# Attention by landmarks and expert layer on one core: q, k and C turned in 32x32 blocks by VectorE instead of by TensorE, scores and v product in 32x32 tiles, the pseudo-inverse carried as I-X, and a new plan of the order

## The chip, the core and the metric

The kernel runs on one core of one Trainium2 chip. The core has five engines that each work through their own queue in order: TensorE (PE in the profile, with its weight loads shown as PEld), VectorE (DVE), ScalarE (ACT), GpSimd (POOL) and SyncE (SP, which here only issues DMAs). TensorE writes its results into PSUM; VectorE and ScalarE read them there. The metric is the device time of one execution in microseconds. The kernel before takes 335.03 us, the median of three runs (333.28, 335.03 and 337.61).

## The reference

There are two parts. The first is an attention in Nyström form over 8 batches, 8 heads, 576 rows and a head size of 64, with m = 32 landmarks; a landmark is the mean of 18 successive rows.

```
q_lm = q.reshape(B, H, m, S // m, D).mean(axis=3)
k_lm = k.reshape(B, H, m, S // m, D).mean(axis=3)
A = sm(q, k_lm); Bm = sm(q_lm, k_lm); C = sm(q_lm, k)     # sm: softmax of the scaled scores
Z = Bm.T / (norm1(Bm) * norminf(Bm) + 1e-06)
for _ in range(6):
    Z = 2 * Z - Z @ Bm @ Z
attn = A @ Z @ C @ v
```

The second is an expert layer over the 4608 rows of 512 values (heads side by side). Each row goes to the one of 8 experts with the highest logit, through `relu(x @ w1[e]) @ w2[e]` (512 to 1024 to 512), and is scaled by its gate probability and by a sigmoid gate. The output is 4608 x 512 in float32.

## The kernel before

**Layout and work per half.** A batch is worked in two halves of four heads (`hf`, 16 halves in all). q, k and v of a half are loaded by one DMA each on SP (L378) into 96 partitions: partition p holds six successive rows of each of the four heads, in four pieces of 1,536 bytes. TensorE turns q and k with an identity matrix (L390: six columns of blocks, 24 transposes of 96x128 a half), and the results are copied out of PSUM by ScalarE or VectorE (`copy_to`, L345 and L351) into `Tk` and `Tq`: on partitions are then 2 rows x 64 of the head size. The sums over the 18 rows of a landmark are taken from `T` (L412 to L424: VectorE in one reduction, L414 and L417, or GpSimd in four additions, L420 to L424), the two partition halves are swapped and added (L347, L351 and L435). That gives `lm`.

The scores of C (L446) and of A (L491) are matmuls on 64x32 tiles of the array: eight calls of 288 columns, each on its own tile. For C: maximum (L452, VectorE), exponential (L455, ScalarE), six transposes of 128 columns on TensorE (L463), a copy out (ECT), and the product with v on 128x32 tiles (L475, 24 calls of 64 columns), scaled into `XW` (L481). For A: a 32x32 block transpose from PSUM by VectorE (L495), maximum (L498), subtraction on GpSimd (L503), exponential (L505), sums and reciprocal (L509, L510), product on GpSimd (L512), and the transpose back into `AT` (L516).

**Work per batch.** B's scores and softmax (L527 to L545), its column sums (L554 to L560), then the pseudo-inverse. It does not form Z; it carries `[X | Y]` per head, 32 + 64 columns, with X in the place of Z·B and Y of Z·C·v: a matmul gives `X·[X | Y]` (L573, eight calls of 96 columns on 32x32 tiles), and VectorE forms `2[X | Y] - X·[X | Y]` (L580 to L585), seven times. Then the logits (L593 to L621), the routing on VectorE (`route1` to `route4`, L637 to L686) with a count over all partitions on TensorE (`count`, L655), and x in bf16, transposed (`xT_all`, L699). The expert that most rows of the batch chose gets its weights by DMAs on GpSimd's queue (L312, L315 and L720, with a cast from float32 to bf16). Then 64 matmul calls `up` a batch (L734, 288 columns, bf16), relu by ScalarE (L343), 40 calls `down` a batch (L749, 512 columns), a scaled copy (L756 or L758) and the store on SP (L761). Rows of other experts are handled afterwards under a condition.

**What sets the order.** Nothing in this part is ordered by hand on the engines. The class `Plan` takes each piece of work as an operation (`P.op`) with the engines that may do it and a cost in nanoseconds for each, what it reads and writes, a tile form for TensorE (`mode`; a change costs `SWITCH` = 95) and a priority, and simulates a schedule once when the program is built. The operations are emitted in the order of their planned start; every engine then runs its own queue in that fixed order and waits wherever an operand is late. Priorities are about the batch number `b` plus a small step; the expert matmuls of batch `b` have `fr = b + 3.5`, so they stand behind the attention of the next three batches where both are ready. Tiles come from small pools (`tag`): three buffers each for q, k and v, two for `T`, two PSUM pairs `S`, two banks `M`, two banks `F` for the expert matmuls, one w1 and one w2 for even and one for odd batches.

Of the kernel before, what the change touches and what calls it, by code (L numbers as in the profile page):

```python
# [22 lines left out]
F32 = mybir.dt.float32  # L23
# [5 lines left out]
ADD = mybir.AluOpType.add  # L29
# [193 lines left out]
def kernel(  # L223
# [23 lines left out]
    PT = 96  # L247
# [5 lines left out]
    SHYF = 300.0  # L253
# [13 lines left out]
    ones = pool.tile([128, 128], F32, name="ones")  # L267
    e8 = pool.tile([128, E], F32, name="e8")
# [15 lines left out]
    t_s3 = tag("s3", 1, [128, HH * PT])  # L284
    t_s9 = tag("s9", 2, [128, 2, 128])
    t_lm = tag("lm", 3, [128, 2, 128])
    t_sw = tag("sw", 1, [128, 2, 128])
    t_EC = tag("EC", 1, [128, 2, U2])
    t_ECT = tag("ECT", 1, [PT, 6, 128])
# [27 lines left out]
    with tc.manual_schedule():  # L317
        nc.vector.memset(ones, 1.0)
# [9 lines left out]
        for hf in range(2):  # L328
            nc.sync.dma_start(out=wgs[hf * D:(hf + 1) * D, :, :E],
                              in_=moe_w_gate[hf * HH * D:(hf + 1) * HH * D].rearrange("(h d) e -> d h e", d=D))  # L330
            nc.sync.dma_start(out=wgs[hf * D:(hf + 1) * D, :, E:],
                              in_=moe_w_output_gate[hf * HH * D:(hf + 1) * HH * D].rearrange("(h d) e -> d h e", d=D))
        nc.vector.tensor_scalar(out=wgs[:, :, E:], in0=wgs[:, :, E:], scalar1=-1.0, scalar2=None, op0=MUL)
# [19 lines left out]

        def turned(T, x):
            if x == "k":
                return T.t.rearrange("p (j n) -> p j n", j=3)
            return T.t.rearrange("p (n j) -> p j n", j=3)

# [6 lines left out]
        xTs, coms = {}, {}  # L365

        def batch(b):
# [4 lines left out]
            vns = []  # L372
            for hf in range(2):
                pr = b + 0.1 * hf
                ns = {}
                for x, src in (("k", k), ("q", q), ("v", v)):
                    n = ns[x] = Val(t_n[x])
                    P.op({"SP": 60}, lambda e, n=n, src=src, hf=hf: nc.sync.dma_start(  # L378
                        out=n.t, in_=src[b, hf * HH:(hf + 1) * HH].rearrange("h (p t) d -> p h (t d)", t=6)),
                        w=[n[0]], prio=pr, lag=2000, load=2300)  # L380
                vns.append(ns["v"])
                Ts = {"q": Val(t_T["q"]), "k": Val(t_T["k"])}
                order = [("k", 0), ("k", 1), ("k", 2), ("q", 0), ("q", 1), ("q", 2)]
                for a in range(3):
                    tp = Val(p_S)
                    two = order[2 * a:2 * a + 2]
                    for i, (x, j) in enumerate(two):
                        def turn(e, x=x, j=j, i=i, tp=tp, n=ns[x]):
                            for h in range(HH):
                                nc.tensor.transpose(tp.t[:, i, h * PT:(h + 1) * PT],  # L390
                                                    in_=n.t[:, h, j * 128:(j + 1) * 128], identity=I128[:PT, :PT])
                        P.op({"PE": 332}, turn, r=[ns[x][0]], w=[tp[i]], hold=[Ts[y] for y, _ in two], mode=(128, 128), prio=pr + .01)
                    if two[0][0] == two[1][0]:
                        x, j = two[0]
                        T = Ts[x]
                        P.op(evac(768), copy_to(lambda T=T, j=j, x=x: turned(T, x)[:, j:j + 2],
                                                lambda tp=tp: tp.t[:, :, :HH * PT]),
                             r=[tp[0], tp[1]], w=[T[j], T[j + 1]], prio=pr + .01)
                    else:
                        for i, (x, j) in enumerate(two):  # L400
                            T = Ts[x]
                            P.op(evac(384), copy_to(lambda T=T, j=j, x=x: turned(T, x)[:, j],
                                                    lambda tp=tp, i=i: tp.t[:, i, :HH * PT]),
                                 r=[tp[i]], w=[T[j]], prio=pr + .01)
                s9 = Val(t_s9)
                for i, x in enumerate("qk"):
                    T = Ts[x]
                    s3 = Val(t_s3)

                    def sums(e, T=T, s9=s9, s3=s3, i=i, x=x):  # L410
                        f = turned(T, x)
                        if e == "DVE":  # L412
                            if x == "k":
                                nc.vector.tensor_reduce(  # L414
                                    s9.t[:, i], f.rearrange("p j (r w) -> p r j w", w=3), axis=XY, op=ADD)
                            else:
                                nc.vector.tensor_reduce(  # L417
                                    s9.t[:, i], T.t.rearrange("p (r w) -> p r w", w=9), axis=X, op=ADD)
                            return
# [14 lines left out]
                def folded(e, lm=lm, s9=s9, sw=sw):  # L434
                    (nc.gpsimd if e == "POOL" else nc.vector).tensor_tensor(lm.t, s9.t, sw.t, op=ADD)  # L435
# [409 lines left out]
```

## Time and profile before

| what | value |
|---|---|
| median of three runs | 335.03 us |
| the profiled execution | 333.46 us, of which span 331.8 us |
| PE busy | 287.8 us (87%) |
| DVE busy | 192.0 us (58%) |
| ACT busy | 174.7 us (53%) |
| POOL busy | 85.2 us (26%) |
| mean granted PE clock | 0.973 |
| read from HBM | 61.90 MB, written 9.44 MB |

"Busy" of an engine is the time in which at least one of its instructions runs; matmuls are pipelined, so a busy PE may still be waiting in part. A group line of the profile gives line, engine, operation, output<-input, shapes, count, then busy time and the mean nanoseconds of one, then the idle time of the engine just before such instructions and what ended it. In the listing by slices the span is cut in 40 equal parts (8.3 us each) and each digit is a busy share in tenths. A line of the timeline gives start and length in us, engine, line and operation, and how many instructions are merged in it. A row of the view by stretches gives the stretch, its length, and the busy time of PE, PEld, DVE, ACT and POOL in it (with instruction counts), then the granted clock, the DMA share and GB/s.

### The profile page before, as it was taken

Reading aid. Unit: us, or ns where it says so; the run is one execution under the profiler, and the core shown is the slowest. Engines: PE = TensorE matmul, PEld = TensorE weight load, DVE = VectorE, ACT = ScalarE, POOL = GpSimd, SP = SyncE. Lnnn points to the kernel's source line nnn. Section 1 sums busy time; section 2 is a strip of 40 time slices with the busy share of each in tenths; the row PEclk is TensorE's granted clock in tenths of the full one; section 3 lists DMA queues with packets and bytes.
Section 4 is the critical chain, followed back from the end, with each engine's and each line's share of the span. In section 5 each row is a group of like instructions: output and inputs, shape, how many; then the busy total and the mean of one; then the engine's idle time right before and its main releaser. Section 6 shows DMA issues by size and latency. Waiting matters only on the chain. (4 is left out here: it accounts for less than half of the span.)

```text
span 331.8 us, 10174 instructions
## 1 busy us (share of the span) xinstructions
PE 287.8 (87%) x4270; PEld 182.8 (55%) x4281; DVE 192.0 (58%) x526; ACT 174.7 (53%) x370; POOL 85.2 (26%) x126
## 2 busy tenths in 40 slices
PE   0576868799979989899978998999999998999994
PEld 0545655566656665657644575666565555454551
DVE  1258928977987388729866669784968626000000
ACT  1344526537845457537654566465764345454542
POOL 1034642237153024214331402330221311010000
PEclk9999779769999999999999999999999999999999
DMA  4999999289999978076730455665000946949103
GB/s 96 247 247 245 250 213 233 49 187 227 229 182 232 261 225 193 9 212 178 167 85 2 134 154 123 139 104 167 2 18 2 219 84 99 177 113 200 51 33 112
DMA packets 33584, 48.95 MB, mean 147 GB/s; under 512 B 2816, under 2 KB 26368, under 8 KB 33536
## 3 DMA queue, kind: packets, MB, share of 16 engines
q1 hardware_dynamic: 25536, 37.79, 44.4%
q0 software_dynamic: 8000, 10.49, 19.7%
q8 instruction: 34, 0.56, 0.7%
q14 instruction: 14, 0.11, 0.1%
HBM read 61.90 MB, written 9.44 MB: 215 GB/s over the span
## 5 line engine op out<-in xcount | busy, mean ns | idle before, releaser
L734 PE MATMUL F<-xT_all,w 128*128 128x288 bf16 x512 | 76.1, 286 | 2.1 <-ACT y L756 1.1
L749 PE MATMUL F<-w,hT 128*128 128x512 bf16 (+1 forms) x310 | 73.2, 380 | 1.0 <-ACT y L756 0.3
L734 PEld LDWEIGHTS <-w 128*128 128x128 bf16 x512 | 47.4, 98 | 24.1 <-issue 11.7
L343 ACT ACTIVATE hT<-F 128x288 bf16<-128x288 f32 x128 | 50.0, 411 | 16.8 <-PE F L734 14.9
L749 PEld LDWEIGHTS <-hT 128*128 128x128 bf16 (+1 forms) x320 | 30.7, 100 | 35.0 <-issue 2.8
L756 ACT ACTIVATE y<-F,co 128x512 f32<-128x512 f32 (+1 forms) x38 | 26.1, 686 | 42.4 <-PE F L749 36.6
L390 PE MATMUL S<-I,nk 96*128 96x96 f32 x192 | 25.2, 275 | 14.2 <-DMA nk<-in_k_dram 11.2
L573 PE MATMUL M<-X 32*32 32x96 f32 x768 | 26.5, 251 | 5.3 <-issue 3.2
L503 POOL TENSOR_TENSOR At<-At,sm 128x576 f32<-128x576 f32 x16 | 18.5, 1156 | 49.1 <-DVE sm L498 27.5
L390 PEld LDWEIGHTS S<-I,nk 96*128 96x128 f32 x192 | 21.1, 160 | 17.1 <-issue 9.0
L345 ACT COPY Tq<-S 128x768 f32<-128x768 f32 (+1 forms) x23 | 22.9, 1004 | 11.1 <-PE S L390 11.1
L390 PE MATMUL S<-I,nq 96*128 96x96 f32 x192 | 24.6, 270 | 2.1 <-DVE Tk L351 1.8
L345 ACT COPY Tk<-S 128x384 f32<-128x384 f32 (+1 forms) x25 | 15.6, 633 | 20.0 <-PE S L390 19.5
L512 POOL TENSOR_TENSOR At<-At,sm 128x576 f32<-128x576 f32 x16 | 18.5, 1159 | 28.2 <-DVE sm L510 10.3
L583 DVE SCALAR_TENSOR_TENSOR X<-X,M 128x192 f32<-128x192 f32 x40 | 13.7, 344 | 19.6 <-PE M L573 19.4
L573 PEld LDWEIGHTS M<-X 32*32 32x32 f32 x768 | 15.7, 105 | 16.7 <-issue 7.8
L417 DVE TENSOR_REDUCE s<-Tq 128x128 f32<-128x1152 f32 x14 | 18.9, 1350 | 8.8 <-ACT Tq L345 8.7
L390 PEld LDWEIGHTS S<-I,nq 96*128 96x128 f32 x192 | 20.4, 156 | 5.7 <-DVE Tk L351 2.4
L345 ACT CAST xT_all<-S 128x576 bf16<-128x576 f32 x28 | 16.7, 641 | 11.3 <-PE S L699 11.2
L455 ACT ACTIVATE EC<-S,sm 128x576 f32<-128x576 f32 x16 | 11.8, 740 | 18.3 <-DVE sm L453 16.7
L435 POOL TENSOR_TENSOR lm<-s,sw 128x256 f32<-128x256 f32 x12 | 8.7, 725 | 41.1 <-ACT sw L345 34.4
L345 ACT COPY ECT<-S 96x768 f32<-96x768 f32 x14 | 11.1, 796 | 14.9 <-PE S L463 14.8
(118 smaller groups left out, 395.0 us busy)
## 6 DMA issues: line engine op xcount, KB each, us to landing
nk<-in_k_dram SPq DMA_DIRECT2D x16, 576.0 KB, 8.8
nq<-in_q_dram SPq DMA_DIRECT2D x16, 576.0 KB, 8.4
nv<-in_v_dram SPq DMA_DIRECT2D x16, 576.0 KB, 8.0
w<-in_moe_w_dram POOLq DMA_DIRECT2D x8, 1024.0 KB
out_dram<-y SPq DMA_DIRECT2D x32, 256.0 KB, 2.7
w<-in_moe_w_dram POOLq DMA_DIRECT2D x8, 512.0 KB
w<-in_moe_w_dram POOLq DMA_DIRECT2D x16, 256.0 KB
out_dram<-y SPq DMA_DIRECT2D x8, 128.0 KB, 2.4
```

The lines of the kernel that those rows point to most:

```text
L343: nc.scalar.activation(out=dst(), in_=src(), func=RELU)
L345: nc.scalar.copy(dst(), src())
L390: nc.tensor.transpose(tp.t[:, i, h * PT:(h + 1) * PT], in_=n.t[:, h, j * 128:(j + 1) * 128], identity=I128[:PT, :PT])
L417: nc.vector.tensor_reduce(s9.t[:, i], T.t.rearrange("p (r w) -> p r w", w=9), axis=X, op=ADD)
L455: P.op({"ACT": 900}, lambda e, pC=pC, EC=EC, st=st: nc.scalar.activation(out=EC.t, in_=pC.t[:, :, :U2], func=EXP, scale=s_a, bias=st.t[:, ...
L503: P.op({"POOL": 1160}, lambda e, At=At, st=st: nc.gpsimd.tensor_tensor(At.t, At.t, b_l(st.t[:, 8:8 + g]), op=SUB), r=[st["ax"]], w=[At[0]] ...
L512: P.op({"POOL": 1160}, lambda e, At=At, st=st: nc.gpsimd.tensor_tensor(At.t, At.t, b_l(st.t[:, 32:32 + g]), op=MUL), r=[st["as"]], w=[At[0 ...
L573: nc.tensor.matmul(pN.t[r_, hf * W:(hf + 1) * W], lhsT=cur.t[r_, hf, :m], rhs=cur.t[r_, hf, :])
L583: nc.vector.scalar_tensor_tensor(out=nxt.t, in0=cur.t, scalar=2.0, in1=p3, op0=MUL, op1=SUB)
L734: nc.tensor.matmul(ph.t[:, :NH], lhsT=w1.t[:, dc, fc * 128:(fc + 1) * 128], rhs=xT.t[:, dc, n * NH:(n + 1) * NH], start=(dc == 0), stop=(d ...
L749: nc.tensor.matmul(py.t[:tk, :], lhsT=hTs[fc].t[:, i * 128:i * 128 + tk], rhs=w2.t[:, fc, :], start=(fc == 0), stop=(fc == FCH - 1))
L756: nc.scalar.activation(out=y.t[:tk], in_=py.t[:tk, :], func=COPY, scale=com.t[:tk, i:i + 1])
```

## The change

- q and k are loaded as 128 partitions (head, landmark) with 18 rows x 64 values each, 4,608 bytes in one piece. VectorE turns them in 32x32 blocks in one instruction each (L391); the head size then lies in two blocks `j` of 32. v is loaded the same way with its two partition halves exchanged, by two DMAs.
- Landmark sums are taken from the loaded rows: batch 0 on TensorE with a stack of 32x32 identities `I32s` (L404, 144 calls a half), later batches on GpSimd in five additions (L414 to L418) or VectorE in one reduction (L412). A 32x32 block transpose gives `lm` (L423 or L427). The swap and the fold go away.
- The scores of C and A become one operation of 32 calls on 32x32 tiles (L443 and L445), accumulated over `j`. C's rows are written two heads further (`o`), so both use different tiles. C's maximum stays on VectorE (L450), its scaling moves to ScalarE (L454).
- C is turned in 32x32 blocks by VectorE (L459) and the v product runs on 32x32 tiles: 72 calls of 64 columns (L468). Its scale is done by ScalarE or VectorE (L479, L481).
- The pseudo-inverse carries `[R | Y]` with R = I - X. The matmul gives `R·[R | Y]` (L565, eight calls) and a second one adds Y through the identity (L568, eight calls of 64 columns); the step is then a plain copy by ScalarE or VectorE (L582, L584). The last step does the Y columns alone.
- AT is written at steps of 18 elements (L506). The gate weights are loaded in an operation of their own, and negated on GpSimd (L386).
- The plan: `fr = b + 1.5`, new costs for loads (2050 for 2300, weights 5000 for 8100) and for the new operations.

In the built order TensorE gets, for 384 transposes of q and k and 96 of C that go away, 288 calls for sums, 1152 instead of 384 for the v product, 512 instead of 256 for the scores and 384 more in the pseudo-inverse. It changes its tile form 136 times instead of 200. The first expert matmul of batch 0 stands a few operations behind the count of batch 0, ahead of the v products of batch 2.

```diff
-    t_n = {x: tag(f"n{x}", 3, [PT, HH, 6 * D]) for x in "qkv"}
-    t_T = {x: tag(f"T{x}", 2, [128, 3 * HH * PT]) for x in "qk"}
+    t_n = {x: tag(f"n{x}", 3, [128, g, D]) for x in "qkv"}
+    t_T = {x: tag(f"T{x}", 2, [128, 2, S]) for x in "qk"}
...
+        nc.vector.tensor_reduce(I32s, I128.rearrange("p (a c) -> p c a", c=m), axis=X, op=ADD)
...
+                    def bring(e, n=n, x=x, src=src, hf=hf):
+                        rows_ = src[b, hf * HH:(hf + 1) * HH].rearrange("h (r t) d -> (h r) t d", t=g)
+                        if x != "v":
+                            nc.sync.dma_start(out=n.t, in_=rows_)
+                            return
+                        for a in range(2):
+                            nc.sync.dma_start(out=n.t[a * D:(a + 1) * D], in_=rows_[(1 - a) * D:(2 - a) * D])
...
-                        def turn(e, x=x, j=j, i=i, tp=tp, n=ns[x]):
-                            for h in range(HH):
-                                nc.tensor.transpose(tp.t[:, i, h * PT:(h + 1) * PT],
-                                                    in_=n.t[:, h, j * 128:(j + 1) * 128], identity=I128[:PT, :PT])
-                        P.op({"PE": 332}, turn, r=[ns[x][0]], w=[tp[i]], hold=[Ts[y] for y, _ in two], mode=(128, 128), prio=pr + .01)
...
+                for x in "kq":
+                    P.op({"DVE": 1370}, lambda e, T=Ts[x], n=ns[x]: nc.vector.transpose(
+                        out=T.t.rearrange("p j (t r) -> p t j r", r=m), in_=n.t.rearrange("p t (j c) -> p t j c", j=2)),
+                        r=[ns[x][0]], w=[Ts[x][0]], prio=pr + .01)
...
+                        def sums_pe(e, n=ns[x], pM=pM, i=i):
+                            for t in range(g):
+                                for h in range(HH):
+                                    r_ = slice(h * m, (h + 1) * m)
+                                    nc.tensor.matmul(pM.t[r_, i * D:(i + 1) * D], lhsT=I32s[r_, :], rhs=n.t[r_, t, :],
+                                                     start=(t == 0), stop=(t == g - 1))
+                        P.op({"PE": 1020}, sums_pe, r=[ns[x][0]], w=[pM[i], s9[i]], mode=(32, 32), prio=pr + .005)
...
+                        nc.gpsimd.tensor_tensor(s3.t, n.t[:, :9], n.t[:, 9:], op=ADD)
+                        nc.gpsimd.tensor_tensor(s3.t[:, :4], s3.t[:, :4], s3.t[:, 4:8], op=ADD)
+                        nc.gpsimd.tensor_tensor(s3.t[:, :2], s3.t[:, :2], s3.t[:, 2:4], op=ADD)
+                        nc.gpsimd.tensor_tensor(s3.t[:, 0], s3.t[:, 0], s3.t[:, 1], op=ADD)
+                        nc.gpsimd.tensor_tensor(s9.t[:, i], s3.t[:, 0], s3.t[:, 8], op=ADD)
+                    P.op({"POOL": 2850, "DVE": 1350}, sums, r=[ns[x][0]], w=[s9[i], s3[0]], prio=pr + .005, shy={"DVE": SHY})
...
+                def scores(e, pC=pC, pA=pA, lm=lm, Ts=Ts):
+                    for n in range(2):
+                        for j in range(2):
+                            for h in range(HH):
+                                r_ = slice(h * m, (h + 1) * m)
+                                o = (h + 2) % HH
+                                nc.tensor.matmul(pC.t[o * m:(o + 1) * m, n, :U2], lhsT=lm.t[r_, 0, j, :],
+                                                 rhs=Ts["k"].t[r_, j, n * U2:(n + 1) * U2], start=(j == 0), stop=(j == 1))
+                                nc.tensor.matmul(pA.t[r_, n, :U2], lhsT=lm.t[r_, 1, j, :],
+                                                 rhs=Ts["q"].t[r_, j, n * U2:(n + 1) * U2], start=(j == 0), stop=(j == 1))
+                P.op({"PE": 1050}, scores, r=[lm[0], Ts["k"][0], Ts["q"][0]], w=[pC[0], pA[0]], hold=[EC, At, st],
+                     mode=(32, 32), prio=pr + .03)
...
+                P.op({"DVE": 780}, lambda e, EC=EC, ECT=ECT: nc.vector.transpose(
+                    out=ECT.t.rearrange("p t r -> p (t r)"), in_=EC.t.rearrange("p a c -> p (a c)")),
+                    r=[EC[0]], w=[ECT[0]], prio=pr + .03)
...
-                    for c in range(6):
-                        t = 2 * (c % 3) + c // 3
+                    for t in range(g):
                         for h in range(HH):
-                            nc.tensor.matmul(pV.t[h * m:(h + 1) * m, :D], lhsT=ECT.t[:, c, h * m:(h + 1) * m],
-                                             rhs=n.t[:, h, t * D:(t + 1) * D], start=(c == 0), stop=(c == 5))
-                P.op({"PE": 850}, pv, r=[ECT[0], ns["v"][0]], w=[pV[0]], hold=[XW], mode=(128, 32), prio=pr + .04)
+                            o = (h + 2) % HH
+                            nc.tensor.matmul(pV.t[h * m:(h + 1) * m, :D], lhsT=ECT.t[o * m:(o + 1) * m, t, :],
+                                             rhs=n.t[o * m:(o + 1) * m, t, :], start=(t == 0), stop=(t == g - 1))
+                P.op({"PE": 1020}, pv, r=[ECT[0], ns["v"][0]], w=[pV[0]], hold=[XW], mode=(32, 32), prio=pr + .04)
...
-                    out=AT.t[:, :S].rearrange("p (u n) -> p n u", n=2), in_=At.t.rearrange("p (n k) r -> p n (k r)", n=2)),
+                    out=AT.t[:, :S].rearrange("p (r t) -> p t r", t=g), in_=At.t),
...
+                            nc.tensor.matmul(pN.t[r_, hf * W + lo:(hf + 1) * W], lhsT=cur.t[r_, hf, :m],
+                                             rhs=cur.t[r_, hf, lo:], start=True, stop=(it == 0))
+                            if it:
+                                nc.tensor.matmul(pN.t[r_, hf * W + m:(hf + 1) * W], lhsT=I32s[r_, :],
+                                                 rhs=cur.t[r_, hf, m:], start=False, stop=True)
...
+                P.op({"ACT": 320, "DVE": 340} if it else {"DVE": 600}, step, r=[pN[0], sb[3]] if it == 0 else [pN[0]],
+                     w=[nxt["x"], nxt["y0"], nxt["y1"]], prio=pr + .05)
...
-            fr = b + 3.5
+            fr = b + 1.5
```

More of the change, by code (lines that the diff above doesn't have):

```diff
@@ L267 @@
     ones = pool.tile([128, 128], F32, name="ones")
+    I32s = pool.tile([128, m], F32, name="I32s")
     e8 = pool.tile([128, E], F32, name="e8")
@@ new lines, in c_rec @@
+                def c_rec(e, st=st):
+                    for a in range(2):
+                        nc.vector.reciprocal(st.t[a * D:(a + 1) * D, 3:4], st.t[(1 - a) * D:(2 - a) * D, 2:3])
+                P.op({"DVE": 280}, c_rec, r=[st[1]], w=[st[2]], prio=pr + .035)
+                def pv_out(e, pV=pV, st=st, hf=hf):
+                    if e == "ACT":
+                        nc.scalar.activation(out=XW.t[:, hf, m:], in_=pV.t[:, :D], func=COPY, scale=st.t[:, 3:4])
+                    else:
+                        nc.vector.tensor_scalar(out=XW.t[:, hf, m:], in0=pV.t[:, :D], scalar1=st.t[:, 3:4],
+                                                scalar2=None, op0=MUL)
@@ L495, in batch @@
+                P.op({"ACT": 260, "DVE": 285}, pv_out, r=[pV[0], st[2]], w=[XW[f"y{hf}"]], prio=pr + .04)
                 P.op({"DVE": 800}, lambda e, pA=pA, At=At: nc.vector.transpose(
```

184 lines of the change are left out of this document (65 added, 119 removed).

## The prediction

> **What bounds the kernel now.** I read the stretches first, cut at the routing of the first and of the last batch (the count matmul L655 starts at 63.6 and 277.7 us), then the slices, the matmul rows of the timeline, and the waits.
>
> ```profile
> 0.00:63.60 63.60, 39.64 (x642) 28.12 (x643) 36.73 (x81) 27.92 (x52) 22.09 (x40) 0.93 0.91 206
> 63.60:277.70 214.10, 200.41 (x3363) 128.58 (x3370) 152.17 (x429) 121.74 (x267) 60.26 (x82) 0.98 0.62 140
> 277.70:331.80 54.10, 47.76 (x267) 26.12 (x270) 3.10 (x18) 25.02 (x53) 2.80 (x4) 0.99 0.46 107
> ```
> Columns: stretch, length, then PE, weight loads, DVE, ACT and POOL busy, clock, DMA share, GB/s. In the middle stretch PE is busy 200 of 214 us, DVE 152, ACT 122: PE sets the pace. The start is set by loads and chains; the end is expert work alone.
>
> ```profile
> PE   0576868799979989899978998999999998999994
> DVE  1258928977987388729866669784968626000000
> PEclk9999779769999999999999999999999999999999
> ```
> PE fills up only after slice 9 (first expert matmul at 79.5 us); its clock dips in slices 4 to 8.
>
> ```profile
> 75.07 0.53 PE L573 MATMUL M<-X 32*32 32x96 f32 x16
> 75.53 0.88 PE L475 MATMUL M<-nv,ECT 96*32 96x64 f32 x48
> 76.34 0.88 PE L390 MATMUL S<-I,nk 96*128 96x96 f32 x8
> 82.96 0.74 PE L699 MATMUL S<-AT,X 32*64 32x288 f32 x16
> 85.03 0.72 PE L446 MATMUL S<-Tk,lm 64*32 64x288 f32 x16
> ```
> An f32 matmul shows as two passes (8 calls, x16); a transpose as one. Passes on different tiles of the array start 7 ns apart; a tile's next pass waits for its last. L475: 48 passes on 4 tiles are 12 rounds; 0.88 less one pass's 0.22, over 11, is 0.060, and 0.056 after the first in the single rows. So I count **rounds**: 0.25 us for 288 columns, 0.136 for 160, 0.083 for 96, 0.056 for 64, 0.03 for 32; a 96-column transpose 0.082, a 128-column one 0.11; expert matmuls 0.1225 (L734) and 0.216 (L749); about 0.09 for a change of tile form.
>
> ```profile
> L573 PE MATMUL M<-X 32*32 32x96 f32 x768 | 26.5, 251 | 5.3 <-issue 3.2
> L417 DVE TENSOR_REDUCE s<-Tq 128x128 f32<-128x1152 f32 x14 | 18.9, 1350 | 8.8 <-ACT Tq L345 8.7
> L503 POOL TENSOR_TENSOR At<-At,sm 128x576 f32<-128x576 f32 x16 | 18.5, 1156 | 49.1 <-DVE sm L498 27.5
> L345 ACT COPY Tq<-S 128x768 f32<-128x768 f32 (+1 forms) x23 | 22.9, 1004 | 11.1 <-PE S L390 11.1
> ```
> The last columns are the idle time of the engine before the group and what ended it. Before L573, the longest chain on PE, that is only 5.3 us in the whole run; the other three rows are prices used below. By rounds the middle holds 185 us of PE work (worked out below), so 29 of its 214 us go in many small waits and in pipeline ends, not in one place.
>
> **The change on PE.** There are 16 halves (8 batches, four heads at a time). Removed: 384 transposes of q and k x 0.082 = 31.5, 96 of C x 0.11 = 10.6, and, by the built orders, 64 of 200 changes of form x 0.09 = 5.8: 47.9 us.
> Added:
> - Scores. Before, C and A take 8 tiles for two rounds each (4 x 0.25 = 1.0 us a half). Now 32 calls of 32 rows lie on 8 tiles: 8 passes per tile, 2.0 us. 16 x 1.0 = 16.0.
> - v product. 72 calls on 4 tiles are 36 rounds instead of 12: 24 x 0.056 x 16 = 21.5.
> - Pseudo-inverse. Five steps gain 4 rounds of 64 columns (0.224), the last has 8 of 64 for 4 of 96 (+0.12): 8 x 1.24 = 9.9.
> - B's scores: 8 rounds of 32 columns for 2: 8 x 0.18 = 1.4.
> - Sums of batch 0: 144 rounds x 0.056 = 8.1, in PE time that is idle now; double at the low clock (there the L475 at 67.33 us took 1.51 instead of 0.88, rounds of 0.107).
> The sum is +0.9 us, +8 at the start: **PE gets no lighter.** The planner holds other numbers (1020 ns for a v product, 1050 for the scores, against 2.0 us each by rounds), so PE will run behind its plan by about 2 us a half.
>
> The Trainium skill, TensorEngine Tiling, Restrictions and Gotchas, Gotcha 1 (PSUM Pressure), says that different row tiles cannot access the same PSUM bank at the same time. Four row tiles of the new v product write one bank; by that rule they would go one after the other (the serial rival below). The trace speaks against it: L573 has just that layout, and its four tiles start 7 ns apart (0.53 us for 16 passes; in series 16 x 0.083 = 1.3).
>
> **VectorE.** Added: 32 turns of 1152 columns. Rows give 0.335 us for 160 and 0.770 for 576 columns, 1.05 ns a column, so 1.37 (between 1.2, columns alone, and 1.54, twice 576): 43.8. 16 turns of C x 0.77 = 12.3; 16 of the landmarks x 0.30 = 4.8; I-X 8 x 0.25 = 2.0. AT is now written at 72-byte steps: between no cost (0.77 now at 8-byte steps) and the half more of ACT's 12-byte copies (1206 against 798 ns); VectorE's own (1188 against 954) is nearest: +0.19 x 16 = 3. Removed: 21 of 25 sums x 1.34 = 28, the evictions of T, C and sw 17.6, most X steps. Adding rows over the built order I get 204 us (+3 for AT) against 209 for before (its rows overlap, busy 192). **VectorE stays level**, and lies beside PE as now; without that cover its 3 us would count.
>
> **ACT, POOL, SP.** ACT loses evictions of T, C and sw (22.9 + 15.8 + 11.1 + 7.2 = 57 us) and gains 39 copies of X at about 0.3 and 32 small operations at 0.2: net -39. POOL's landmark sum becomes 1.16 + 0.73 + 0.49 + two of 0.4 = 3.2 us, 24 times (77) for 20 us of old sums and 11.5 of folds: 85 becomes 130 of 320 us, hidden; but an At operation may stand behind a sum for 3.2 us. v comes by two DMAs: 16 more issues of 0.3 to 0.6 on SP, which idles. The four gate loads still lead SP's queue; their negation (0.18 us) leaves VectorE for POOL, where 0.4 us beside the first loads cost nothing. Loads of 4.6 KB rows for 1.5 KB: taken equal (2.3 us each in the start's queue).
>
> **Where the work lies.** Experts move from priority b+3.5 to b+1.5, so a batch's FFN comes about two batches sooner, between the attention of the next ones. Their weight loads (three DMAs for w1, one for w2 a batch) keep their place behind the routing on POOL's queue; each waits for the buffer of the batch before last, and in the built order that batch's last use stands before the count or a few matmuls behind it, so POOL hardly stands. The outputs wait on SP's queue among the loads of q, k and v, as now. By rounds on the built orders the middle goes from 185.2 us (FFN 87.7, transposes 29.5, scores 12.0, v 8.7, inverse 16.3, rest 15.7, switches 15.3) to 202.6 (FFN 100.8, scores 24.0, v 24.2, inverse 24.9, rest 17.0, switches 11.7). The end after the last count falls from 44.3 to 31.3.
>
> **The sum.**
> - Start. The first C max is at 23.05 now. Then: k lands at 9.1, its sums cold 3.9, q's 3 more, turn 0.3, scores 2.1 = 18.6. From there VectorE has as much to do until the count as now (33 us of rows now, 35 after), and that takes 40.5 us now: 59 (63.6 now).
> - Middle. 202.6 plus waits. Everything beside PE gets less or equal and PE gets more, so waits shrink: between 11 (if the others keep the 214 us) and 29 (as now). I take 20, the midpoint, since no row is nearer to one end. The first experts' weights: issued 67.2, used 79.5 now; only 5.7 us of PE work lie between count and first use, so 4 us more: 226.
> - End. 54.1 now for 44.3; 4.6 of it are after the last matmul. 31.3 x 49.5 / 44.3 + 4.6 = 39.3.
> Span 59 + 226 + 39.3 = 324.3; with the 1.7 us around it (333.46 for 331.8): **326.0 us**. The profiled run lies 1.6 under the median 335.03.
>
> **Rivals.**
> 1. *The waits stay in proportion.* 202.6 x 214.1 / 185.2 = 234, plus 4: 59 + 238 + 39.3 + 1.7 = 338. For it: PE, ACT and DVE still stand in fixed orders planned with other times. Against: ACT loses 39 us.
> 2. *The others set the pace.* The middle keeps its 214: 314 us. For it: VectorE's level sum. Against: PE then must be busy 95%.
> 3. *Slower: each half's chain gets longer than the plan knows.* Place: landmarks, scores, max, exp, turn, v product, run once per half; 2.3 us of PE time in it are not in the plan, and VectorE's max and turn stand in order before other work. Price: if 1 us of each of the middle's 14 halves is not covered, 14 us on rival 1: 352, at half of that 345. It decides (over 341.7) from 0.27 us a half on. For it: VectorE's queue often stands at L452 or L495 already (5.1 us before L452). Against: slack grows when PE is late.
> 4. *Row tiles in series.* 144 passes x 0.056 = 8.1 instead of 2.0 us: 16 x 6.1 = 97 more, 423 us.
>
> **The numbers.** Chances: forecast 0.40 (its own range 317 to 328, for waits of 11 to 22 us), rival 2 0.11, rival 1 0.30, rival 3 0.16, rival 4 0.03. Two per cent, about what a measurement can tell here, puts the bounds at 328.3 and 341.7. Faster: 0.40 + 0.11 = 0.51; same: 0.30; slower: 0.19. The range 311 to 346 leaves out the lower half of rival 2, the upper half of rival 3, and rival 4: 0.17.
>
> **What would show it.** Right: scores 2.0 to 2.2 us and the v product 2.0 to 2.2 us per half in the timeline; k and q turns of 1.37; first count near 59, last near 285; PE over 92% busy between. Wrong: a v product near 1.0 (the plan's number) or 8 us; first expert matmul later than 76; VectorE's queue standing at the scores; waits in the middle over 30 us; AT turns over 1.2.

## The result and the profile after

The changed kernel takes 374.06 us, the median of four runs (371.57 to 374.56); the kernel before, run beside it, 336.32 (333.28 to 338.94). The ratio is 1.114, with a 95% interval of 1.103 to 1.125: slower by 11%, where 326 us were predicted and 346 was the upper end of the range. Ratios leave out runs over 1.5% longer than the fastest of the same kernel; medians count every run. The profiled execution of the changed kernel has a span of 372.7 us, 40.9 more than before.

The same three stretches, cut at the first and at the last count matmul (now L654, at 77.2 and 333.1 us). Columns: stretch, length, busy us of PE, weight loads, DVE, ACT and POOL, clock, DMA share, GB/s.

```profile
0.00:77.20 77.20, 44.15 (x1761) 36.22 (x1762) 41.51 (x81) 13.10 (x39) 31.85 (x58) 0.85 0.56 164
77.20:333.10 255.90, 223.35 (x5373) 147.35 (x5366) 156.73 (x391) 110.08 (x289) 95.73 (x139) 0.96 0.51 126
333.10:372.70 39.60, 34.00 (x194) 18.74 (x194) 3.08 (x18) 18.18 (x39) 2.79 (x4) 1.00 0.51 114
```

The start is 13.6 us longer, the middle 41.8, and the end 14.5 shorter. From the first parts of the page:

```profile
span 372.7 us, 16256 instructions
...
PE 301.5 (81%) x7320; PEld 202.3 (54%) x7321; DVE 201.3 (54%) x488; ACT 141.3 (38%) x366; POOL 130.4 (35%) x200
...
PE   1575566675798958899999998849998969999994
...
PEclk9969959788889989999999999998999989999999
```

PE is busy 13.7 us longer than before, but that leaves 27 us of the 41 open: PE now also has holes late in the run, 5, 4 and 6 tenths at slices 15, 27 and 33 (counted from 1), where it had 8, 9 and 9 before. What stands before each kind of matmul says why. These are the waits of PE; "issue" means that the engine waited for nothing that the profile shows:

```profile
PE M L468 <- issue: 19.5, 9, 3.7
PE M L404 <- DMA nk<-in_k_dram: 8.1, 1, 8.1
PE M L565 <- issue: 6.6, 8, 1.9
PE M L404 <- issue: 6.6, 3, 4.2
PE S L445 <- issue: 5.7, 3, 2.7
```

Columns: us in all, times, longest. Before, the largest such line was 3.2 us, once, at the pseudo-inverse. Now the v product (L468) alone has 19.5. One of these places in the timeline:

```profile
131.29 1.91 PE L468 MATMUL M<-nv,ECT 32*32 32x64 f32 x120
136.93 0.24 PE L468 MATMUL M<-nv,ECT 32*32 32x64 f32 x2 [3.73 <-issue]
```

The v product of one half is 144 passes on operands that are all there, and it breaks off in the middle for 3.73 us. Last, the DMA queue that brings instructions; the first fence is the kernel before, the second the changed one (packets, MB, share):

```profile
q8 instruction: 34, 0.56, 0.7%
```
```profile
q8 instruction: 58, 0.95, 1.0%
```

A packet is 16 KB. The page counts 8551 matmuls and weight loads of TensorE before and 14641 after; at 256 to a packet that is 33.4 and 57.2, and the queue brought 34 and 58. So these packets carry TensorE's instructions; the strings below show the 256 directly. I set the start of every packet beside every place where PE starts nothing for over 0.8 us without a wait on a semaphore (a **standing place**, counted from start to start). Before there is one, 3.4 us. In the changed kernel there are 19, 42.3 us in all, and every one ends 1.26 to 1.56 us after a packet has landed (in 13 it lands within the place, in six up to 0.45 us ahead of it). The one above: a packet starts at 134.50, has landed at 135.43, PE goes on at 136.93. Eight of the 19 stand before a v product (20.8 us), three before scores (7.4), three before the sums of batch 0 (7.2), five before the pseudo-inverse (6.9). The clearest string of them lies at the start, with packets at 27.16, 30.77, 34.39 and 38.14 us, one in 3.6 to 3.8 us.

So 38.9 of the 40.9 us are standing places that came in: in size, the whole difference. Size is no proof, since PE may lose elsewhere what it would gain here; hence the experiments.

### The profile page after: what moved, and what is told of

It is laid out like the page before. It is cut to its first block, busy times and chain, and to the rows that moved or that the text cites. A ratio compares the mean times of both kernels' runs of the same rounds, so it can differ in the third digit from the quotient of the medians.

```text
span 372.7 us, 16256 instructions
## 1 busy us (share of the span) xinstructions
PE 301.5 (81%) x7320; PEld 202.3 (54%) x7321; DVE 201.3 (54%) x488; ACT 141.3 (38%) x366; POOL 130.4 (35%) x200
## 5 line engine op out<-in xcount | busy, mean ns | idle before, releaser
L468 PE MATMUL M<-nv,ECT 32*32 32x64 f32 x2304 | 42.3, 224 | 20.6 <-issue 19.5
L468 PEld LDWEIGHTS M<-nv,ECT 32*32 32x32 f32 x2304 | 38.0, 110 | 23.8 <-issue 21.5
L445 PE MATMUL S<-Tq,lm 32*32 32x288 f32 x512 | 43.5, 458 | 5.7 <-issue 5.7
L493 POOL TENSOR_TENSOR At<-At,sm 128x576 f32<-128x576 f32 x16 | 18.6, 1161 | 81.2 <-DVE sm L488 68.1
L443 PE MATMUL S<-Tk,lm 32*32 32x288 f32 x512 | 42.3, 459 | 1.7 <-issue 0.9
L565 PE MATMUL M<-X 32*32 32x96 f32 (+1 forms) x768 | 34.6, 249 | 10.5 <-issue 4.9
L565 PEld LDWEIGHTS M<-X 32*32 32x32 f32 x768 | 21.6, 105 | 18.7 <-issue 7.2
L568 PE MATMUL M<-X,I32s 32*32 32x64 f32 x768 | 31.3, 218 | 0.0
L502 POOL TENSOR_TENSOR At<-At,sm 128x576 f32<-128x576 f32 x16 | 18.6, 1162 | 31.8 <-DVE sm L500 29.4
L582 ACT COPY X<-M 128x192 f32<-128x192 f32 (+1 forms) x39 | 12.0, 309 | 45.7 <-PE M L568 45.6
L445 PEld LDWEIGHTS S<-Tq,lm 32*32 32x32 f32 x512 | 22.6, 117 | 8.9 <-issue 7.3
L568 PEld LDWEIGHTS M<-X,I32s 32*32 32x32 f32 x768 | 24.8, 108 | 3.3 <-issue 3.3
L443 PEld LDWEIGHTS S<-Tk,lm 32*32 32x32 f32 x512 | 22.4, 116 | 6.5 <-issue 3.4
L391 DVE STREAM_TRANSPOSE Tk<-nk 128x1152 f32<-128x1152 f32 x16 | 21.6, 1352 | 5.5 <-DMA nk<-in_k_dram 5.5
L479 ACT ACTIVATE XW<-M,sm 128x64 f32<-128x64 f32 x15 | 4.7, 313 | 52.5 <-PE M L468 52.5
```

The source lines that it names most:

```text
L391: P.op({"DVE": 1370}, lambda e, T=Ts[x], n=ns[x]: nc.vector.transpose(out=T.t.rearrange("p j (t r) -> p t j r", r=m), in_=n.t.rearrange("p ...
L443: nc.tensor.matmul(pC.t[o * m:(o + 1) * m, n, :U2], lhsT=lm.t[r_, 0, j, :], rhs=Ts["k"].t[r_, j, n * U2:(n + 1) * U2], start=(j == 0), sto ...
L445: nc.tensor.matmul(pA.t[r_, n, :U2], lhsT=lm.t[r_, 1, j, :], rhs=Ts["q"].t[r_, j, n * U2:(n + 1) * U2], start=(j == 0), stop=(j == 1))
L468: nc.tensor.matmul(pV.t[h * m:(h + 1) * m, :D], lhsT=ECT.t[o * m:(o + 1) * m, t, :], rhs=n.t[o * m:(o + 1) * m, t, :], start=(t == 0), sto ...
L493: P.op({"POOL": 1160}, lambda e, At=At, st=st: nc.gpsimd.tensor_tensor(At.t, At.t, b_l(st.t[:, 8:8 + g]), op=SUB), r=[st["ax"]], w=[At[0]] ...
L502: P.op({"POOL": 1160}, lambda e, At=At, st=st: nc.gpsimd.tensor_tensor(At.t, At.t, b_l(st.t[:, 32:32 + g]), op=MUL), r=[st["as"]], w=[At[0 ...
```

## The experiments

**Theory S**: TensorE's instructions arrive at no more than 256 in about 3.7 us, some 14 ns each. An f32 matmul takes four (two passes, each with a weight load). A v product of 72 calls is 288 instructions in 2.2 us of work, faster than they come. **Rival W**: the work on 32x32 tiles itself, in columns, costs more than I counted. **Rival P**: the new plan is at fault.

### Fewer instructions, the same columns; and the reverse

> The changed kernel, but the v product takes two neighbouring steps t in one matmul of 128 columns with the weights of the even one: 36 matmuls a half in place of 72, each twice as wide, so TensorE streams exactly as many columns with half the instructions (the v product then weighs the odd steps wrongly). Theory S (supply of instructions): in the changed kernel's trace TensorE stands 42 us in 19 places where nothing that it waits for is late, and in each of them one 16 KB packet of instructions lands; the before has one such place of 3.4 us. 144 instructions fewer a half are 2304 in all, 9 packets, and the v product is the densest string of them (8 of the 19 places, 21 us). S expects these places to go: 345 to 358 us. Rival W (TensorE's own work in 32x32 tiles, counted in columns, is what made the change slow): no column is saved, so 366 to 376 us.

```diff
-                    for t in range(g):
+                    for t in range(0, g, 2):
...
-                            nc.tensor.matmul(pV.t[h * m:(h + 1) * m, :D], lhsT=ECT.t[o * m:(o + 1) * m, t, :],
-                                             rhs=n.t[o * m:(o + 1) * m, t, :], start=(t == 0), stop=(t == g - 1))
+                            nc.tensor.matmul(pV.t[h * m:(h + 1) * m, :2 * D], lhsT=ECT.t[o * m:(o + 1) * m, t, :],
+                                             rhs=n.t[o * m:(o + 1) * m, t:t + 2, :], start=(t == 0), stop=(t == g - 2))
```

Measured: 355.16 us (350.00 to 356.77), 19 below the changed kernel, with 49 packets and 7 standing places of 15.9 us. In its waits the v product has nearly left:

```profile
PE M L404 <- issue: 7.9, 3, 4.4
...
PE M L468 <- issue: 2.4, 2, 1.8
```

The columns are the same and 19 us are gone, which lies in S's band: W falls for this part. 26.4 us of standing went, the span fell by 19.4; a part of what is saved is lost to other waits (PE now waits 8.5 us for expert weights, where it waited 2.6).

> The kernel before, with the same columns in more instructions: each score matmul of 288 columns as three of 96, each v-product matmul of 64 columns as two of 32. Nothing else moves; 56 matmuls more a half, each issued as 4 instructions: 224 a half, 3584 in all, 14 packets of 256. Theory S (supply of instructions): standing places with a packet in them appear at these lines, 345 to 360 us. Rival W (columns): 331 to 339 us, as before, apart from a little for the shorter matmuls.

```diff
-                                             rhs=turned(T, "k")[t2 * D:(t2 + 1) * D, :, h * PT:(h + 1) * PT])
+                            for j in range(3):
+                                nc.tensor.matmul(pC.t[h * m:(h + 1) * m, t2, j * PT:(j + 1) * PT],
...
+                    for u, c in ((u, c) for u in range(2) for c in range(6)):
...
+                            nc.tensor.matmul(pV.t[h * m:(h + 1) * m, u * m:(u + 1) * m], lhsT=ECT.t[:, c, h * m:(h + 1) * m],
```

Measured: 380.99 us (ratio 1.138, 1.130 to 1.147), worse than S expected, and not by packets: 48 packets, 9 standing places of only 16.9 us. My edit had a second effect. It put three thirds of a score one behind the other on the same tile, and the two score lines grew from 12.4 and 12.5 us to 37.8 and 33.9. So the order was turned:

> As e2_before_split (the kernel before with 3584 more instructions for the same columns), but the order is turned: in the scores the third of the columns is the outermost loop, so that neighbouring matmuls go to different tiles, as before; in e2 three in a row went to the same 64x32 tile, and the two score lines took 69 us where they had taken 24, which is more than its standing places (16.8 us in 9) explain. If neighbours on one tile are what cost the rest: the two lines 24 to 32 us, the standing places about as in e2, in all 342 to 358 us. Rival S alone (all of e2's 46 us came from the packets, the places just not being shown as waits): 370 to 382 us. Rival W (columns alone): 331 to 339.

```diff
-                    for h in range(HH):
+                    for j, h in ((j, h) for j in range(3) for h in range(HH)):
                         for t2 in range(2):
-                            nc.tensor.matmul(pC.t[h * m:(h + 1) * m, t2, :U2],
+                            nc.tensor.matmul(pC.t[h * m:(h + 1) * m, t2, j * PT:(j + 1) * PT],
```

Measured: 363.32 us (ratio 1.087, 1.075 to 1.098), 5 above the expected band; the two score lines 15.7 and 17.1 us, near the upper end of what was expected, but 13 standing places of 27.5 us where about e2's were expected; again 48 packets. The scores of A, first with neighbours on one tile (e2), then turned (e8); busy us, mean ns, then idle time before them:

```profile
L493 PE MATMUL S<-Tq,lm 64*32 64x96 f32 x768 | 33.9, 247 | 2.9 <-issue 2.9
```
```profile
L491 PE MATMUL S<-Tq,lm 64*32 64x96 f32 x768 | 17.1, 282 | 10.5 <-issue 10.4
```

In e8 the line is busy half as long and stands 10.5 us instead: once the tiles overlap, it is instructions that are missing. The kernel before, with one standing place, gets 27 us slower by 3584 more instructions for the same columns.

### The cost by itself

> The kernel before, with three strings of matmuls that nobody reads behind its last one, where no load is under way and they wait for nothing: A 720 of 32x32 by 64 columns in f32 (2880 instructions, 11 packets), B 360 by 128 columns in f32 (the same columns, 1440 instructions), C 720 by 64 columns in bf16 (half the columns of A, 1440 instructions). In each, four tiles in turn. Theory S (supply of instructions): the densest chain of packets in the changed kernel's trace is one in 3.6 us, 256 instructions, so A 36 to 46 us, B 18 to 23, C 18 to 23. Rival W (columns): the v product of 18 rounds took 2.0 us where nothing stood, so 180 rounds are 20 us: A 20, B 20, C 10. If loads are what slows the packets, A comes out between: 22 to 32.

```diff
+        for src, cols in ((None, 64), (None, 128), (c16, 64)):
+            for i in range(180 * 64 // cols):
+                for h in range(HH):
+                    r_ = slice(h * m, (h + 1) * m)
+                    nc.tensor.matmul(p_M.tiles[0][r_, :cols], lhsT=(ones if src is None else src)[r_, :m],
+                                     rhs=(I128 if src is None else src)[r_, :cols], start=True, stop=True)
```

The kernel with the strings ran once (420.30 us); they are timed in its trace. Measured: A 41.1 us, B 21.3, C 20.6. That is S on all three; W fits B alone. The head of string A in the timeline:

```profile
331.56 3.98 PE L774 MATMUL M<-I,ones 32*32 32x64 f32 x268
336.86 1.99 PE L774 MATMUL M<-I,ones 32*32 32x64 f32 x128 [1.31 <-issue]
340.86 1.99 PE L774 MATMUL M<-I,ones 32*32 32x64 f32 x128 [2.01 <-issue]
```

128 passes with their 128 weight loads are one packet: 1.99 us of work, 2.01 us of standing, then the next. And the queues under string A (331.6 to 372.6 us):

```profile
DMA packets 212, 0.52 MB, mean 13 GB/s; under 512 B 33, under 2 KB 33, under 8 KB 201
...
q8 instruction: 10, 0.16, 1.5%
```

Nothing but the last outputs is moving, and still there are only 10 packets in 41 us, 3.93 us apart. The loads are not what slows them. C has the instructions of B with half the columns of A, and takes B's time.

### Undoing one part each

> The changed kernel with the v product as it was before: the exponentials turned by 6 TensorE transposes and an eviction of 768 columns, then 24 matmuls of 96 rows by 64 columns; v comes in its old layout (three loads of 32 partitions), and k's columns are read in an order to match. Scores, landmarks, turns of q and k, pseudo-inverse and plan stay changed. Computes the reference. Instead of 288 instructions a half it has 96 and the transposes' few: about 2800 fewer in all, 11 packets. Theory S: 340 to 355 us. Rival W (columns): the v product's rounds go (my count: 21.5 us), 16 x 0.66 us of transposes come back: 359 to 365 us.

```diff
+                    for c in range(6):
+                        nc.tensor.transpose(pE.t[:96, c // 3, (c % 3) * 128:(c % 3 + 1) * 128],
+                                            in_=EC.t[:, c // 3, (c % 3) * 96:(c % 3 + 1) * 96], identity=I128)
...
+                            nc.tensor.matmul(pV.t[h * m:(h + 1) * m, :D], lhsT=ECT.t[:, c, o * m:(o + 1) * m],
+                                             rhs=n.t[:, h, c * D:(c + 1) * D], start=(c == 0), stop=(c == 5))
```

Measured: 337.30 us (ratio to before 1.010, 1.002 to 1.019). Undoing one part, the v product in 72 calls with its turn and its load, brings back 37 of the 38 us. 47 packets; the four standing places left (9.3 us) all lie ahead of the first count. W's 359 to 365 is far off; S's 340 to 355 is missed too, by 3. The shares of single parts do not add up: e5 and e6 below bring back 8 and 10 us more. The granted clock, 0.940 in the changed kernel for 0.973 before, does not make the difference: at 0.946 e4 takes 337.30 us, at 0.963 e2 takes 380.99.

> The changed kernel with one part undone: batch 0's landmarks are summed by GpSimd and VectorE like the other batches', not by TensorE. Computes the reference. 2304 instructions, 9 packets, fewer in the first 30 us. Theory S (supply of instructions, measured by the strings at 3.65 us a packet): the 18.8 us of the sums' line, 7.2 of them standing, go from the start, GpSimd's sums come instead; the first count at 62 to 70 (77), the rest as before: 358 to 369 us. Rival (what is saved at the start is lost behind it, as from 12 us at the first count 4 to 6 were left at the end between e4 and b3): 367 to 374.

```diff
-    PESUM = 1
+    PESUM = 0
```

Measured: 366.02 us (361.88 to 375.84; ratio to before 1.088, 1.078 to 1.098): 8 below the changed kernel, in S's band but too scattered to exclude the rival's 367 (the two quickest runs, 361.88 and 363.97, are below it). First count at 70.8 us, not 62 to 70. The expectation counts the instructions double: 288 calls, 576 passes in the trace, are 1152 instructions and 4.5 packets, not 9; 54 packets came for 58. So do those of e6, b3 and b2: the pseudo-inverse's 384 calls are 6 packets, not 12.

> The changed kernel with one part undone: the pseudo-inverse squares X as before, one matmul a tile and 2X - X*X on VectorE. Computes the reference. 768 matmuls, 3072 instructions, 12 packets fewer, in 48 strings; in the changed kernel's trace the two lines hold TensorE 49 us, the line before 32, and 6.9 us stand there in 5 places. Theory S: 17 us of TensorE's time go, and v products find more packets landed: 345 to 360 us. Rival (the steps' chain on VectorE is what sets the pace of the pseudo-inverse, as it was before, and comes back): 366 to 376.

```diff
-                            if it:
-                                nc.tensor.matmul(pN.t[r_, hf * W + m:(hf + 1) * W], lhsT=I32s[r_, :],
-                                                 rhs=cur.t[r_, hf, m:], start=False, stop=True)
...
+                        nc.vector.scalar_tensor_tensor(out=nxt.t[:, :, lo:], in0=cur.t[:, :, lo:], scalar=2.0,
+                                                       in1=p3[:, :, lo:], op0=MUL, op1=SUB)
```

Measured: 363.86 us (ratio to before 1.083, 1.071 to 1.094): 10 less, 4 above S's band and below the rival's. Packets fell to 52, standing only to 35.9 us: the v products still stand.

> e4_v_old (the changed kernel with the v product as before), and batch 0 sums its landmarks on GpSimd and VectorE like the other batches, not on TensorE: 576 matmuls, 2304 instructions, 9 packets fewer, all in the first 30 us. Computes the reference. Theory S: in e4 the sums' line held TensorE 20 us, 7 of them standing; GpSimd's sums of 3.2 us each come instead: first count at 58 to 66 (e4: 72), 322 to 333 us. Rival (the start hangs on the loads and on VectorE, and the sums are beside it): 334 to 340.

The edits are those of e4 and e5. Measured: 333.21 us (330.46 to 339.94), at the edge between both bands: undecided (two runs near 330.6 lie in S's band, 335.56 in the rival's, 339.94 at its end). The first count came forward from 72.0 to 60.6 as S said, the span from 335.0 to 329.2 only.

> b3_v_old_nosum, and the pseudo-inverse squares X as before (2X - X*X on VectorE, one matmul a tile in each of 7 steps) in place of I-X (two matmuls a tile, steps copied by ScalarE or VectorE): 768 matmuls, 3072 instructions, 12 packets fewer, and 42 VectorE steps more that ScalarE shared. Computes the reference. Theory S: 5 to 15 us under b3_v_old_nosum, 312 to 328. Rival (packets fit already once the v product is lighter, and VectorE's queue holds the steps up): as b3 or up to 6 us slower.

The edits are those of e4, e5 and e6. Measured: 328.33 us (ratio to before 0.980, 0.972 to 0.989), 36 packets, one standing place of 0.9 us. It is 4.9 below b3, at the edge of S's band (312 to 328), and b3 is scattered: by how much the pseudo-inverse counts here is undecided. What remains of the change is the turns of q and k on VectorE, the scores on 32x32 tiles, the sums off TensorE, AT's steps, C's scaling on ScalarE and the plan.

> b2_v_pinv_old_nosum (turns of q and k on VectorE, scores in 32x32 tiles, v product and pseudo-inverse as before, sums on GpSimd and VectorE: 328.3 us), and the planner is told the durations that the traces show: scores 2050 ns and not 1050, sums 3200 and 2100 and not 2850 and 1350, turn of AT 1240 and not 800. Computes the reference. If wrong costs make TensorE's queue stand at the wrong work: 318 to 326 us; if the order hardly matters now: 326 to 332.

```diff
-                P.op({"PE": 1050}, scores,
+                P.op({"PE": 2050}, scores,
...
-                    P.op({"POOL": 2850, "DVE": 1350}, sums,
+                    P.op({"POOL": 3200, "DVE": 2100}, sums,
```

Measured: 329.48 us (ratio 0.983, 0.975 to 0.991): the planner's wrong costs for scores, sums and AT cost nothing there.

### The plan

> The changed kernel with the three constants of the plan as they were before (experts' work due at b+3.5 and not b+1.5, loads taken at 2300 and 8100 ns and not 2050 and 5000). Theory S: the order of the work may spread the short matmuls a little otherwise, but as many instructions have to come: 362 to 382 us. Rival P (the new plan is what made it slow: first count at 77 where it was 64, and TensorE's queue standing at work whose input is late): 335 to 350 us.

```diff
-    LOAD = 2050.0
-    WLOAD = 5000.0
+    LOAD = 2300.0
+    WLOAD = 8100.0
...
-            fr = b + 1.5
+            fr = b + 3.5
```

Measured: 388.33 us (ratio to before 1.163, 1.153 to 1.174). Rival P is refuted in this form, the old plan is 14 us worse; S's band is missed by 6. PE stands 33.3 us in 16 places, less than in the changed kernel: what the old plan loses is lost in other waits.

> The kernel before with the three constants of the new plan alone (experts' work due at b+1.5, loads taken at 2050 and 5000 ns). In the changed kernel the new constants took 13 us off (385.7 with the old ones to 372.7). If the plan is worth something by itself: 322 to 331 us. If it fits only the changed work: 333 to 345.

The same edit the other way round, in the kernel before. Measured: 364.28 us (ratio 1.094, 1.086 to 1.102), outside both bands: the plan's constants alone cost the kernel before 28 us, with no packet more (34) and one standing place of 2.3 us.

In the next six only `fr` is changed, in f1 the loads' figures too:

> The changed kernel with only the experts' due time as before (b+3.5), loads taken at the new figures. If the due time makes the 13 us that e3_old_plan lost: 380 to 392 us. If the loads' figures do: 366 to 378 us.

> The kernel before with only the experts' due time as in the change (b+1.5). If the due time makes the 28 us that e11_before_new_plan lost: 358 to 368 us. If the loads' figures do: 332 to 342 us.

> b2_v_pinv_old_nosum (328.3 us, one standing place) with the plan's three constants as before. The new constants took 13 us off the changed kernel and put 28 us on the one before. Theory Q (the sign hangs on the supply of instructions: dense strings want the experts' long matmuls between them, so that packets land meanwhile, and without dense strings the old plan is better): 305 to 320 us. Rival V (it hangs on the turns on VectorE and the new scores, which b2 keeps): 335 to 350 us.

> b2_v_pinv_old_nosum with the experts' work due at b+2.5, half way between the two plans. Theory Q: between b2 and f1_b2_old_plan, 312 to 328 us. Rival V: 328 to 340 us.

> The kernel before with the experts' work due at b+2.5 and nothing else: the control for f2_b2_due_mid (316.7 us). If f2's gain is the due time's: 314 to 322 us here too. If it comes from the VectorE turns and scores that b2 keeps of the change: 330 to 345 us.

> The changed kernel with the experts' work due at b+2.5 and nothing else. Due at b+3.5 it took 388, at b+1.5 374. Theory S: the packets stay whatever the order, 30 us or more standing: 360 to 385 us. If its slowness was the plan after all: 318 to 340 us.

Measured, us, by the experts' due time (b+3.5 and b+2.5 or b+1.5; the loads' figures of each kernel's own, but in b2 at b+3.5 the old ones):

| kernel | b+1.5 | b+2.5 | b+3.5 |
|---|---|---|---|
| before | 345.12 (f4) | 343.44 (g1) | 334 to 337 |
| changed | 374.06 | 377.64 (g2) | 388.17 (f3) |
| b2 | 328.33 | **316.70** (f2) | 335.58 (f1) |

In the changed kernel the due time makes all of e3's loss (f3). In the one before it makes about 11 of the 28 us (f4: 345.12 for 334.21 beside it), between its two expectations; the rest comes when the loads' figures are added (never run alone). In g2 PE still stands 38.3 us in 19 places, as S said: no due time tried saves the changed kernel. That the sign of the plan hangs on the packets (theory Q) failed at f1, where 305 to 320 were expected and V's 335 to 350 came; the rival V failed at f2, where Q's 312 to 328 came. Each kernel has a due time of its own that suits it; by what mechanism is **not settled**.

f2 beats both kernels: 316.70 us, ratio to before 0.946 (0.938 to 0.954). The control g1 shows that this is not the due time alone, which makes the kernel before slower (ratio 1.027, 1.018 to 1.036); g1 keeps the old loads' figures, f2 has the new ones. From its page:

```profile
span 316.5 us, 10691 instructions
...
PE 264.7 (84%) x4525; PEld 165.3 (52%) x4537; DVE 212.7 (67%) x517; ACT 138.9 (44%) x336; POOL 120.9 (38%) x185
PE   0065867768878989899969999999999999999994
```

PE is busy 23 us less than before (287.8), as q and k are no longer turned on it, and from slice 22 on it has no hole but the end.

## Why the prediction was wrong, point by point

The step that failed is the part "the change on PE". It priced TensorE's new calls in **rounds**, by the columns that they stream, from rows of a kernel in which instructions nearly always kept up, and carried that over to strings in which they do not. It counted passes and forms, 0.056 us for a round, and never the instructions. The two things that would have told were on the page: one standing place of 3.2 us "issue" before L573, in a fence of the prediction, where it was read as "only 5.3 us", and the instruction queue's 34 packets for 10174 instructions. The working gave +0.9 us for PE, +8 at the start, and put the supply of instructions at nothing; the places where PE stands for it grew by 38.9 us. In the sum it shows as the waits of the middle: 20 us were taken and 4 for the first experts' weights, and 53 came (255.9 less the 202.6 by rounds), 24.6 of them standing places.

By subtraction the rest of the sum comes out near. Each stretch less its own standing places:

| stretch | predicted | measured | standing | less standing |
|---|---|---|---|---|
| start | 59 | 77.2 | 17.8 | 59.4 |
| middle | 226 | 255.9 | 24.6 | 231.3 |
| end | 39.3 | 39.6 | 0 | 39.6 |

That is arithmetic and not a run. In e1, which keeps every column, 0.73 us came off the span for each us of standing removed (19.4 for 26.4), in e5 0.61 (6.4 for 10.5). At e1's rate the 42.3 us are worth some 31, an estimate, and would leave a span of about 342, not 324. No run here has the changed kernel's work without the limit, so whether the rest of the sum held is open. Three slips in my sum do not matter: its own terms give 18.4 for 18.6 at the first scores, 226.6 for 226 and 39.6 for 39.3, in all 326.8 us.

- *Scores and v product 2.0 to 2.2 us*: right where they are not broken off: the shortest v product takes 2.21 us, the shortest scores 2.17. Broken off, a v product took up to 6.9, seven of the 16 over 3.8.
- *PE over 92% busy in the middle*: wrong, 223.35 of 255.9 are 87%. *First expert matmul not later than 76*: wrong, 90.2. *VectorE's queue standing at the scores*, named as a sign of being wrong, came: 16.4 us before C's maximum (L450) for 5.1 before, all of it waiting for TensorE's scores. *First count near 59, last near 285*: wrong, 77.2 and 333.1.
- *The planner's own numbers* (1020 and 1050 ns for 2.0 us each): a true remark without weight; b4 corrected the scores and gained nothing.
- *VectorE level*: not quite, 201.3 for 192.0 busy us, +9. Turns of q and k as said (1.37 taken, 1.35 came). Two prices were low: I took +0.19 us for AT written at 72-byte steps, with 1.16 as the bound, and 1.34 for the strided sum.

```profile
L391 DVE STREAM_TRANSPOSE Tk<-nk 128x1152 f32<-128x1152 f32 x16 | 21.6, 1352 | 5.5 <-DMA nk<-in_k_dram 5.5
L506 DVE STREAM_TRANSPOSE AT<-At 128x576 f32<-128x576 f32 x16 | 19.9, 1241 | 1.8 <-POOL At L502 1.7
L412 DVE TENSOR_REDUCE s<-nq 128x64 f32<-128x1152 f32 x3 | 6.3, 2106 | 0.0
```

  AT costs 0.47 us more, not 0.19, over the bound; the sum 0.77 more, but only four times (the fourth is k's).
- *ACT -39, POOL 85 to 130*: ACT fell by 33 (174.7 to 141.3), POOL is right (130.4).
- *The end by 15 us shorter through the new due time*: right in size, but it is no gain by itself: e11 has an end of 36.4 us and takes 364.
- *Rivals*. The slower rival (345 to 352) had the sign, not the place: what breaks off is TensorE's own strings, the v product first, not the chain around them. Row tiles in series (423): refuted. The Trainium skill, TensorEngine Tiling (Array Packing), Restrictions and Gotchas, Gotcha 1 (PSUM Pressure), says that row tiles cannot access the same PSUM bank at the same time; string A has four row tiles on one bank and streams 128 passes in 1.99 us, where one after the other would be 7.2 by my 0.056 a pass. Read as a cost in time, the rule does not agree with this trace.

## What to carry to other kernels

Price each string of TensorE work twice, by columns and by instructions: in these strings a packet of 256 came every 3.6 to 3.9 us, so one of several hundred instructions that averages under 14 ns each can stand. Not each does: of the 16 v products of 288 instructions seven took over 3.8 us, and two ran in 2.21. An f32 matmul is four instructions and a bf16 one two. Cutting K = 96 into 32x32 tiles made the string three times as long, 288 instructions for 96, and no less dense: 2.21 us are 7.7 ns each, the 0.88 us before 9.2. An "issue" before matmuls whose operands are there, and the packets of the instruction queue, are the two lines to read first. And when a change brings a plan along, try the plan on both kernels.

## What the runs showed of the hardware that I had not expected

- Instruction packets: 3.93 us apart under a string that consumes them in 1.99 us (e7, string A), with next to nothing else moving, and PE goes on about 1.5 us after one has landed. The average is no problem: 58 packets in 372.7 us are one in 6.4; the bursts are.
- Neighbouring matmuls on one tile: three in a row on a 64x32 tile made the same columns 17.7 us dearer than in turn over the tiles (380.99 for 363.32 us, e2 and e8).
- A 32x32 block transpose by VectorE of 576 columns takes 763 ns when written in a row (L459) and 1241 at 72-byte steps (L506).
